# A startup ordered by hand for each engine up to the eighth decoded tile, with its loads in another order

## The chip, the cores and the metric

One core of one Trainium2 chip. The metric is the device time of one execution in microseconds; the median of several runs is compared. A profiled execution gives a trace of every instruction on TensorE (PE, with its weight loads PEld), VectorE (DVE), ScalarE (ACT), GpSimd (POOL) and SyncE (SP), whose queue issues most DMAs.

## What is computed

Packed attention (32 packs attend to 576 keys, then 576 queries attend to the 32 packed rows), then two feed-forward layers, Mish and ELU. In float32 with float64 weights:

```python
def sm_attn(qq, kk, vv):
    s = scale * np.matmul(qq, kk.transpose(0, 1, 3, 2))
    s = s - np.max(s, axis=-1, keepdims=True)
    a = np.exp(s)
    a = a / (np.sum(a, axis=-1, keepdims=True) + 1e-09)
    return np.matmul(a, vv)
p_packed = sm_attn(p, k, v)                 # q, k, v: (4, 8, 576, 64), p: (4, 8, 32, 64)
out = sm_attn(q, p_packed, p_packed)
...
x = attn_out.transpose(0, 2, 1, 3).reshape(2304, 512)
h = x @ w_in                                # 512 x 2048
g = h * np.tanh(sp)                         # sp = log1p(exp(h)), Mish
x = g @ w_out                               # 2048 x 512
...                                         # second layer: the same with ELU
```

## The kernel before

**Weights.** Weights arrive as pairs of 32-bit words, in raw tiles of 128 x 1024 words (512 KB). `decode` (L129) turns a tile into float32 in steps: s0 rebiases one word of each pair on ACT (L147), s1 to s3 shift and merge the bits on DVE (L150, L155, L160), s4 splits the result into a high part on ACT (L175, names ending in h) and a low part on DVE (L179, names ending in l). Each product is then three matmuls: high x high, high x low, low x high. Tiles of w1i, the first layer's first matrix, are not split: they go to w1v, and when a pair of them is done, POOL writes the pair to DRAM for later batches (L167).

**Attention.** Batch 0 runs in the startup, batches 1 to 3 between the matmuls of the batch ahead. The steps are: transposes of keys (hk, DVE L236), `scores1` (sc: PE L256, row maxima L270 on DVE, exponentials L276 on ACT), `transpose_a1` (ta: PE L300, copies L226), `packed` (pk: PE L325, then L338, L349 or L347, and L226 into pt), transposes of queries (hq, L236), and `scores2` (s2): PE L366, transposes L380, maxima and differences L387 and L388, exponentials L389 on ACT, sums and norms L393 to L396, transposes back L403, then the split into a2h (ACT L175) and a2l (DVE L177).

**Fold.** The packed rows are multiplied into the first weight matrix: `fold(b, c)` (PE L428, split by L175 and L179 into gh and gl) needs the four w1i tiles of column c and pt of batch b. It takes the place of the second attention product.

**First layer.** `gemm1` (L459 to L461, six matmuls of 288 columns a unit) multiplies folded weights by a2h and a2l; Mish is L468 on ACT, its split L469 on ACT and L470 on DVE; `gemm2` (L487 to L489, twelve matmuls a unit) multiplies by w1o and runs two units (LAG) behind. A batch has 32 units. Units 0 to 3 need fold column 0, units 4 to 7 column 1, units 8 to 15 both again for the other half of the tokens, units 16 to 19 column 2, units 20 to 23 column 3. Unit n of gemm2 needs w1o tile kk of its number in the same way (kk 0 to 7 in the first 16 units).

**What sets the order.** The framework schedules by priority: instructions have the priority of the order in which they are written, and an engine takes the ready one with the highest, by a model of their durations. Then each engine runs its list in order. In the startup the attention steps are put ahead by `high_priority(60)`, and `filler(m)` (L679) issues m decode steps between them, 65 in all (13 tiles). Behind the startup, `mixture1` writes for each unit gemm1, Mish, decode steps up to DEC1[0] + (i + 1) x DEC1[1] / 32 tiles, attention and fold steps, and gemm2. F0 lists the units at which batch 0's folds of columns 1, 2, 3 are begun. The order of the w1 tiles is `w1seq`: w1i column 0, then by ORD w1o 0, w1i column 1 rows 0, 2, 1, 3, w1o 2, 3, 1, then 4 to 7, then columns 2 and 3 each with its four w1o tiles. The second layer (`mixture2`) begins at about 500 us; its first eight tiles are decoded in mixture1 at PACE2 steps a unit.

**Loads.** p on ACT's queue, k on SP, q of heads 0 to 3 on ACT's queue (8 transfers), v of two groups, two tiles, v of the others, three tiles, q of the other heads on SP (8), four tiles; one more tile with each tile that filler begins.

## Time and profile before

| | before |
|---|---|
| median of 3 runs | 838.66 us (837.78 to 840.06) |
| profiled execution | 838.91 us, of which the span of the trace is 836.8 |
| PE busy | 778.2 us, 93% of the span |
| DVE busy | 438.1 us, 52% |
| ACT busy | 348.1 us, 42% |
| granted TensorE clock, mean | 0.958 |

A page of the profile gives the busy time of each engine, the span in 40 slices, the DMA queues, the chain of work that ended last, and the costliest groups of instructions. Of the first 5 slices (105 us) the page's PE line shows 3, 5, 3, 8 and 9 tenths. Beside the page the trace answers questions on stretches: busy time by window, instructions in order of time, groups of instructions by line, and waits. A line such as `68.47 0.40 PE L487 MATMUL ... [2.19 <-ACT w1oh L175]` reads: at 68.47 us, 0.40 us long, on PE, from line 487, after 2.19 us of idle time that ended when ACT's line 175 wrote w1oh.

### The profile page before, as it was taken

How to read it: one execution, taken by the hardware profiler on the slowest of the kernel's cores; microseconds unless marked ns; L12 is line 12 of the kernel's file. 1: busy time of each engine (PE TensorE's matmuls, PEld its weight loads, DVE VectorE, ACT ScalarE, POOL GpSimd, SP SyncE). 2: the span in 40 equal slices, each digit the busy share in tenths (PEclk: the TensorE clock that was granted, in tenths of full speed). 3: DMA queues.
4: the chain of work that ended last, by engine and by line, in shares of the span. 5: the costliest groups of instructions: out<-in, count | busy, mean ns of one | idle time of the engine just before them, and what ended most of it. 6: DMA issues, size and time to landing. Idle time of an engine off the chain costs nothing. (4 is left out here: it accounts for less than half of the span.)

```text
span 836.8 us, 12979 instructions
## 1 busy us (share of the span) xinstructions
PE 778.2 (93%) x5172; PEld 669.6 (80%) x5172; DVE 438.1 (52%) x860; ACT 348.1 (42%) x674; POOL 14.3 (2%) x30
## 2 busy tenths in 40 slices
PE   3538989999999999999988999999999999999997
PEld 3217969889898997999976887888888888888886
DVE  3889886833564236374359984423343334242342
ACT  1365755655363737474356543312232223221222
POOL 0000000000000000000000000000000000000000
PEclk8558989999999999999999999999999999999999
DMA  8994674263326235030045512200020001000000
GB/s 192 281 409 152 210 214 144 95 174 58 104 85 186 47 90 198 34 126 30 26 174 179 176 53 71 82 1 0 1 76 13 0 1 51 13 1 1 26 26 25
DMA packets 86043, 80.00 MB, mean 96 GB/s; under 512 B 63712, under 2 KB 68320, under 8 KB 85984
## 3 DMA queue, kind: packets, MB, share of 16 engines
q1 hardware_dynamic: 76704, 69.16, 26.9%
q0 software_dynamic: 2432, 8.91, 2.9%
q10 hardware_dynamic: 6848, 1.11, 0.9%
q8 instruction: 40, 0.66, 0.3%
q14 instruction: 19, 0.16, 0.1%
HBM read 65.54 MB, written 13.63 MB: 95 GB/s over the span
## 5 line engine op out<-in xcount | busy, mean ns | idle before, releaser
L488 PE MATMUL acc<-gl,w1oh 128*128 128x288 f32 x512 | 152.4, 300 | 1.4 <-DVE gl L470 1.3
L489 PE MATMUL acc<-gh,w1ol 128*128 128x288 f32 x512 | 151.7, 298 | 0.9 <-DVE w1ol L179 0.9
L487 PE MATMUL acc<-gh,w1oh 128*128 128x288 f32 x512 | 148.5, 299 | 2.2 <-ACT w1oh L175 2.2
L549 PE MATMUL h<-yh,w2ih 128*128 128x512 f32 (+1 forms) x320 | 117.8, 372 | 7.3 <-DVE t L555 5.8
L550 PE MATMUL h<-yl,w2ih 128*128 128x512 f32 (+1 forms) x320 | 119.3, 373 | 0.3 <-DVE yl L177 0.3
L551 PE MATMUL h<-yh,w2il 128*128 128x512 f32 (+1 forms) x320 | 119.0, 372 | 0.0
L572 PE MATMUL o<-w2oh,gh 128*128 128x512 f32 x288 | 112.4, 390 | 1.1 <-ACT ob L224 0.7
L573 PE MATMUL o<-w2ol,gh 128*128 128x512 f32 x288 | 112.2, 390 | 0.0
L574 PE MATMUL o<-w2oh,gl 128*128 128x512 f32 x288 | 108.2, 389 | 0.0
L470 DVE TENSOR_TENSOR gl<-t,gh 128x288 fp32r<-128x288 f32 x128 | 57.9, 454 | 94.5 <-ACT gh L469 93.8
L488 PEld LDWEIGHTS acc<-gl,w1oh 128*128 128x128 f32 x512 | 97.4, 190 | 7.1 <-DVE gl L470 3.7
L487 PEld LDWEIGHTS acc<-gh,w1oh 128*128 128x128 f32 x512 | 96.3, 191 | 6.2 <-ACT w1oh L175 2.4
L489 PEld LDWEIGHTS acc<-gh,w1ol 128*128 128x128 f32 x512 | 97.5, 191 | 3.9 <-issue 2.6
L553 ACT ACTIVATE t<-h 128x512 f32<-128x512 f32 (+1 forms) x80 | 42.3, 552 | 138.2 <-PE h L551 133.7
L554 DVE TENSOR_SCALAR t<-t 128x512 f32<-128x512 f32 (+1 forms) x80 | 31.4, 399 | 122.0 <-ACT t L553 121.5
L468 ACT ACTIVATE t<-h 128x288 f32<-128x288 f32 x128 | 52.2, 409 | 100.2 <-PE h L461 97.0
L459 PE MATMUL h<-a2h,gh 128*128 128x288 f32 x256 | 77.3, 304 | 16.9 <-ACT a2h L175 15.9
L460 PE MATMUL h<-a2l,gh 128*128 128x288 f32 x256 | 77.0, 301 | 1.4 <-DVE a2l L177 1.4
L175 ACT ACTIVATE gh<-t 128x512 fp32r<-128x512 f32 (+1 forms) x80 | 46.6, 587 | 73.9 <-DVE t L555 38.5
L461 PE MATMUL h<-a2h,gl 128*128 128x288 f32 x256 | 76.7, 301 | 0.0
L549 PEld LDWEIGHTS h<-yh,w2ih 128*128 128x128 f32 x320 | 60.7, 190 | 19.5 <-DVE t L555 7.4
L177 DVE TENSOR_TENSOR gl<-t,gh 128x512 fp32r<-128x512 f32 (+1 forms) x80 | 50.1, 636 | 39.2 <-ACT gh L175 38.5
(96 smaller groups left out, 1098.4 us busy)
## 6 DMA issues: line engine op xcount, KB each, us to landing
w1r<-w_dr SPq DMA_DIRECT2D x24, 512.0 KB, 4.3
raw_w1i<-in_moe_w_in_dram SPq DMA_DIRECT2D x16, 512.0 KB, 6.8
raw_w1o<-in_moe_w_out_dram SPq DMA_DIRECT2D x16, 512.0 KB, 8.3
raw_w2i<-in_moe_w_in_dram SPq DMA_DIRECT2D x16, 512.0 KB, 4.3
raw_w2o<-in_moe_w_out_dram SPq DMA_DIRECT2D x16, 512.0 KB, 4.6
k<-in_k_dram SPq DMA_DIRECT2D x16, 288.0 KB, 6.4
y_dr<-y POOLq DMA_DIRECT2D x16, 288.0 KB, 2.5
out_dram<-ob SPq DMA_DIRECT2D x18, 256.0 KB, 2.0
```

The lines of the kernel that those rows point to most:

```text
L459: nc.tensor.matmul(out=hp, lhsT=wh, rhs=xh, start=(kt == 0), stop=False)
L460: nc.tensor.matmul(out=hp, lhsT=wh, rhs=xl, start=False, stop=False)
L461: nc.tensor.matmul(out=hp, lhsT=wl, rhs=xh, start=False, stop=(kt == 1))
L487: nc.tensor.matmul(out=o, lhsT=wh[:, cs], rhs=gh, start=first, stop=False)
L488: nc.tensor.matmul(out=o, lhsT=wh[:, cs], rhs=gl, start=False, stop=False)
L489: nc.tensor.matmul(out=o, lhsT=wl[:, cs], rhs=gh, start=False, stop=last)
L549: nc.tensor.matmul(out=hp, lhsT=wh, rhs=xh, start=(i == 0), stop=False)
L550: nc.tensor.matmul(out=hp, lhsT=wh, rhs=xl, start=False, stop=False)
L551: nc.tensor.matmul(out=hp, lhsT=wl, rhs=xh, start=False, stop=(i == 3))
L572: nc.tensor.matmul(out=o, lhsT=gh[:, ts], rhs=wh, start=(kk == 0), stop=False)
L573: nc.tensor.matmul(out=o, lhsT=gh[:, ts], rhs=wl, start=False, stop=False)
L574: nc.tensor.matmul(out=o, lhsT=gl[:, ts], rhs=wh, start=False, stop=(kk == NK - 1))
```

## The change

- The startup is written inside `manual_schedule` for PE, DVE, ACT and SP: these engines take its instructions in the order in which they are written. `high_priority` and `filler` go. POOL is not in it.
- The order itself is written out. The transpose of p comes first on DVE, then keys, scores1 with both exponentials, and decode steps of tiles 0 to 3 (w1i column 0) between the steps of ta, pk and hq; then scores2; fold 0; tiles 4 to 7 (w1o 0 to 3) between and behind the norms.
- The tiles keep their plain order (no ORD): w1i column 0, w1o 0 to 3, w1i column 1, w1o 4 to 7, and so on. Eight are decoded in the startup, not 13.
- Loads: p on ACT's queue; then all on SP: k, all of v, four tiles, all of q, four tiles, two more.
- DEC1 goes from [14, 26] to [9, 38], F0 from [0, 12, 17] to [3, 12, 16], PACE2 from 9 to 10.
- `split` is divided into `split_hi` and `split_lo`, decode's s4 into s4 (high) and s5 (low). For batch 0 both a2h are written before both a2l. The instructions stay the same.

```diff
-    ORD=[4, 8, 10, 9, 11, 6, 7, 5, 12, 13, 14, 15],
-    DEC1=[14, 26],
-    F0=[0, 12, 17],
+    DEC1=[9, 38],
+    F0=[3, 12, 16],
...
-    PACE2=9,
+    PACE2=10,
...
             else:
+                split_hi(t.bitcast(F32), wt[key][0][:, r % 2, :], 1.0 / WSCALE)
+
+        def s5():
+            if not whole:
                 hi, lo = wt[key]
-                split(t.bitcast(F32), hi[:, r % 2, :], lo[:, r % 2, :], 1.0 / WSCALE)
-
-        return [s0, s1, s2, s3, s4]
+                split_lo(t.bitcast(F32), hi[:, r % 2, :], lo[:, r % 2, :], 1.0 / WSCALE)
+
+        return [s0, s1, s2, s3, s4, s5]
...
+        ] if b else [
+            lambda: exps(0),
+            lambda: exps(1),
+            lambda: (norm(0), back(0, 0)),
+            lambda: (norm(1), back(1, 0)),
+            lambda: (back(0, 1), back(1, 1)),
         ]
...
-    w1seq[4:16] = [w1seq[i] for i in ORD]
...
-        load_kt(q, qt_in, 0, 0, "q", nc.scalar)
-        load_vt(0, 0)
-        load_w1(2)
-        load_vt(0, 1)
-        load_w1(3)
-        load_kt(q, qt_in, 0, 1, "q")
+        for kt in range(2):
+            load_vt(0, kt)
         load_w1(4)
...
+        for kt in range(2):
+            load_kt(q, qt_in, 0, kt, "q")
+        load_w1(4)
+        load_w1(LEAD)
...
+        dec = [decode(*w1dec.popleft()) for _ in range(8)]
...
         order = [
-            hk[0][0], hk[1][0], hk[2][0], hk[3][0], sc[0][0], sc[0][1], sc[1][0], sc[1][1], 2, sc[0][2], sc[1][2],
-            ta[0][0], ta[0][1], ta[1][0], ta[1][1], 4, pk[0][0], pk[0][1], pk[0][2], pk[1][0], pk[1][1], pk[1][2],
-            6, hq[0][0], hq[1][0], hq[2][0], hq[3][0], s2[0], s2[1], s2[2], s2[3], s2[4], 8, f0[0], f0[1],
-            s2[5], s2[6], 45,
+            hk[0][0], hk[1][0], hk[2][0], hk[3][0], sc[0][0], sc[0][1], sc[1][0], sc[1][1],
+            *parts(0, 0), *parts(1, 0), sc[0][2], ta[0][0], ta[0][1], sc[1][2], ta[1][0], *parts(0, 1, 2),
+            ta[1][1], *parts(2, 0), *parts(3, 0), pk[0][0], *parts(0, 3, 4, 5), pk[0][1], pk[1][0], *parts(1, 1, 2), pk[0][2],
+            pk[1][1], *parts(1, 3, 4, 5), pk[1][2], *parts(2, 1, 2, 3, 4, 5), hq[0][0], hq[1][0], *parts(3, 1, 2, 3, 4, 5),
+            hq[2][0], hq[3][0], s2[0], s2[1], s2[2], f0[0], s2[3], s2[4], f0[1], *parts(4, 0), s2[5],
+            *parts(5, 0), s2[6], *parts(4, 1, 2, 3, 4), s2[7],
+            *parts(5, 1, 2, 3, 4), *parts(4, 5), *parts(6, 0), *parts(6, 1, 2, 3, 4), *parts(5, 5),
+            *parts(7, 0), *parts(7, 1, 2, 3, 4), *parts(6, 5), *parts(7, 5),
         ]
         for o in order:
-            if isinstance(o, int):
-                filler(o)
-            else:
-                with tc.high_priority(P['HP']):
-                    o()
-        while micro:
-            filler(1)
+            o()
...
-    startup()
+    with tc.manual_schedule(engines={e.engine for e in (nc.tensor, nc.vector, nc.scalar, nc.sync)}):
+        startup()
```

Here `parts(n, i, ...)` are the steps i of tile n, and `s2[7]` is the new last step of scores2 (both a2l).

## Rows read from the trace of the kernel before

**Rows 1.** Windows: window, length, busy (instructions) by engine, PEclk, DMA share, GB/s.

```profile
54.70:76.00 21.30, 16.69 (x88) 13.58 (x89) 21.30 (x41) 13.81 (x27) 1.63 (x2) 0.70 0.88 300
76.00:89.00 13.00, 13.00 (x122) 12.19 (x121) 12.65 (x28) 9.25 (x21) 0.54 (x1) 1.00 0.11 43
89.00:112.00 23.00, 22.99 (x203) 20.78 (x202) 19.06 (x43) 17.58 (x36) 0.64 (x2) 1.00 0.67 233
112.00:127.20 15.20, 11.57 (x140) 8.65 (x139) 11.07 (x24) 5.69 (x13) 0.96 (x2) 0.78 0.84 210
127.20:300.00 172.80, 171.69 (x1592) 153.52 (x1591) 87.36 (x187) 90.22 (x186) 4.33 (x8) 1.00 0.39 108
```

**Rows 2.** Timeline, 10 to 21 us: start, length, engine, line, operation, [idle before].

```profile
10.37 0.78 DVE L236 STREAM_TRANSPOSE kT<-k 128x576 f32<-128x576 f32 x1 [1.46 <-DMA k<-in_k_dram]
11.08 1.20 DVE L674 STREAM_TRANSPOSE pT<-pr 128x1024 f32<-128x1024 f32 x1
12.33 2.30 PE L256 MATMUL pm<-kT,pT 32*32 32x288 f32 x64 [5.01 <-DVE pT L674]
...
19.95 0.65 ACT L147 ACTIVATE raw_w1i<-raw_w1i 128x512 f32<-128x512 f32 x1 [17.92 <-DMA raw_w1i<-in_moe_w_in_dram]
20.63 0.43 DVE L150 TENSOR_SCALAR dec<-raw_w1i 128x512 int32<-128x512 int32 x1 [4.18 <-ACT raw_w1i L147]
```

**Rows 3.** Timeline, from the second scores to the first gemm2.

```profile
34.74 2.22 PE L366 MATMUL pm<-qT,pt 64*32 64x288 f32 x32 [5.61 <-DVE qT L236]
...
39.44 0.85 DVE L380 STREAM_TRANSPOSE x<-pm 128x288 f32<-128x288 f32 x2
...
47.12 1.41 DVE L393 TENSOR_REDUCE sm<-x 128x18 f32<-128x576 f32 x2 [3.47 <-ACT x L389]
...
58.01 0.76 DVE L177 TENSOR_TENSOR a2l<-a2t,a2h 128x576 fp32r<-128x576 f32 x1
...
63.62 0.55 PE L487 MATMUL acc<-gh,w1oh 128*128 128x288 f32 x2
```

**Rows 4.** Decode: groups by form up to 60 us; gl; windows of dec (DVE, ACT).

```profile
L155 DVE SCALAR_TENSOR_TENSOR dec<-raw_w1i,dec 128x512 int32<-128x512 int32 x8 | 5.4, 683 | 0.1
L160 DVE SCALAR_TENSOR_TENSOR w1v<-raw_w1i,dec 128x512 int32<-128x512 int32 x8 | 5.3, 683 | 0.0
L150 DVE TENSOR_SCALAR dec<-raw_w1i 128x512 int32<-128x512 int32 x8 | 3.3, 419 | 6.2 <-ACT raw_w1i L147 6.2
...
L179 DVE SCALAR_TENSOR_TENSOR w1ol<-dec,w1oh 128x512 fp32r<-128x512 f32 x1 | 0.7, 687 | 0.0
...
L470 DVE TENSOR_TENSOR gl<-t,gh 128x288 fp32r<-128x288 f32 x128 | 57.9, 454 | 94.5 <-ACT gh L469 93.8
...
0.00:60.00 60.00, 16.86 (x31) 0.61 (x1) 0.61 0.97 289
47.10:58.10 11.00, 4.93 (x9) 0.61 (x1) 0.50 1.03 406
```

**Rows 5.** SP's queue: two timeline rows, and what the first v waited for.

```profile
10.19 0.38 SPq L200 DMA_DIRECT2D v<-in_v_dram  x1
...
23.38 7.21 SPq L213 DMA_DIRECT2D q<-in_q_dram  x8
...
SPq L200 <- DMA pr<-in_p_dram: 7.6, 1, 7.6
```

**Rows 6.** Timeline of PE, a wait in gemm2 and the start of unit 4 of gemm1.

```profile
68.47 0.40 PE L487 MATMUL acc<-gh,w1oh 128*128 128x288 f32 x1 [2.19 <-ACT w1oh L175]
...
76.07 0.29 PE L459 MATMUL h<-a2h,gh 128*128 128x288 f32 x1
76.20 0.29 PE L460 MATMUL h<-a2l,gh 128*128 128x288 f32 x1
```

**Rows 7.** Timeline of PE, two neighbouring matmuls of gemm2 at 122 us.

```profile
122.03 0.44 PE L488 MATMUL acc<-gl,w1oh 128*128 128x288 f32 x1
122.27 0.44 PE L489 MATMUL acc<-gh,w1ol 128*128 128x288 f32 x1
```

More of the change, by code (lines that the diff above doesn't have):

```diff
@@ L31 @@
     EVA='va',
-    HP=60,
     WARM=16,
@@ L168, in s4, with split_hi, split_lo @@
             else:
+                split_hi(t.bitcast(F32), wt[key][0][:, r % 2, :], 1.0 / WSCALE)
+        def s5():
+            if not whole:
                 hi, lo = wt[key]
-                split(t.bitcast(F32), hi[:, r % 2, :], lo[:, r % 2, :], 1.0 / WSCALE)
-        return [s0, s1, s2, s3, s4]
-    def split(val, hi, lo, factor=1.0):
+                split_lo(t.bitcast(F32), hi[:, r % 2, :], lo[:, r % 2, :], 1.0 / WSCALE)
+        return [s0, s1, s2, s3, s4, s5]
+    def split_hi(val, hi, factor=1.0):
         nc.scalar.activation(out=hi, in_=val, func=ACTF.Copy, scale=factor)
+    def split_lo(val, hi, lo, factor=1.0):
         if factor == 1.0:
@@ L181, in split @@
             )
+    def split(val, hi, lo, factor=1.0):
+        split_hi(val, hi, factor)
+        split_lo(val, hi, lo, factor)
     def reload_w1i(c):
@@ L396, in norm, with back @@
             nc.vector.tensor_tensor(out=x[s], in0=x[s], in1=sm.to_broadcast([128, NB, NP]), op=ALU.mult)
-        def back(s):
+        def back(s, part=None):
+            if part == 1:
+                split_lo(x["t", s], *x["hl", s])
+                return
             if s == 0:
@@ L404, in back @@
             hi, lo = (y[b][:, s].rearrange("p e s -> p (e s)") for y in (A2h, A2l))
-            split(t, hi, lo)
+            split_hi(t, hi)
+            if part is None:
+                split_lo(t, hi, lo)
+            x["t", s], x["hl", s] = t, (hi, lo)
         return [
@@ L617 @@
     LAG = 2
-    ORD = P['ORD']
     def interleave(name):
@@ L666, in startup @@
             load_heads(k, kt_in, 0, g, "k", nc.sync)
-        load_kt(q, qt_in, 0, 0, "q", nc.scalar)
-        load_vt(0, 0)
-        load_w1(2)
-        load_vt(0, 1)
-        load_w1(3)
-        load_kt(q, qt_in, 0, 1, "q")
-        load_w1(4)
-        nc.vector.transpose(
-            out=pT.rearrange("p g x k -> p (g x k)"), in_=pr.rearrange("p g d -> p (g d)")
-        )
-        micro = deque()
-        def filler(m):
-            for _ in range(m):
-                if not micro and w1dec:
-                    micro.extend(next_w1())
-                    load_w1(1)
-                if micro:
-                    micro.popleft()()
+        for kt in range(2):
+            load_vt(0, kt)
+        load_w1(4)
+        for kt in range(2):
+            load_kt(q, qt_in, 0, kt, "q")
+        load_w1(4)
+        load_w1(LEAD)
         at = attention_steps(0)
@@ L690, in startup, with parts @@
         f0 = fold(0, 0)
-        order = [
-            hk[0][0], hk[1][0], hk[2][0], hk[3][0], sc[0][0], sc[0][1], sc[1][0], sc[1][1], 2, sc[0][2], sc[1][2],
-            ta[0][0], ta[0][1], ta[1][0], ta[1][1], 4, pk[0][0], pk[0][1], pk[0][2], pk[1][0], pk[1][1], pk[1][2],
-            6, hq[0][0], hq[1][0], hq[2][0], hq[3][0], s2[0], s2[1], s2[2], s2[3], s2[4], 8, f0[0], f0[1],
-            s2[5], s2[6], 45,
+        dec = [decode(*w1dec.popleft()) for _ in range(8)]
+        def parts(n, *which):
+            return [dec[n][i] for i in which]
+        nc.vector.transpose(
+            out=pT.rearrange("p g x k -> p (g x k)"), in_=pr.rearrange("p g d -> p (g d)")
+        )
+        order = [
+            hk[0][0], hk[1][0], hk[2][0], hk[3][0], sc[0][0], sc[0][1], sc[1][0], sc[1][1],
[6 more added lines that the diff above has]
+            *parts(7, 0), *parts(7, 1, 2, 3, 4), *parts(6, 5), *parts(7, 5),
         ]
         for o in order:
-            if isinstance(o, int):
-                filler(o)
-            else:
-                with tc.high_priority(P['HP']):
-                    o()
-        while micro:
-            filler(1)
+            o()
     class Track:
```

## The prediction

> **What bounds the kernel now.** I read the time by stages first. From 127.2 us to 300 us TensorE (PE) is busy for 171.69 of 172.80 us at the granted clock 1.00 [rows 1]: from there on the end is fixed by PE's work, which the change leaves as it is. (The one later edit, PACE2 from 9 to 10, goes with one more step for each decoded tile, so 9/5 = 1.8 tiles for each unit become 10/6 = 1.67, for eight tiles in all; I cost it at nothing, half a unit of PE cover.) So the change is worth what it moves PE's state at about 127 us, no more.
>
> Before that point the bound is VectorE (DVE). It is busy for 21.30 of 21.30 us from 54.7 to 76, for 12.65 of 13.00 to 89, then for 19.06 of 23.00 and 11.07 of 15.20 [rows 1]: no idle time up to 76, and 0.35 + 3.94 + 4.13 = 8.4 us from there to 127.2.
>
> Then I read the startup as a chain in order of time. Scores of batch 0 start at 12.33, behind the transposed packs pT at 11.08. DVE then loses 4.18 us at 20.63, in front of a decode step that waits for ScalarE (ACT), which had itself stood 17.92 us in front of the first weight tile [rows 2]. The second scores start on PE at 34.74 and last 2.22, to 36.96, but DVE transposes them only at 39.44; the row sums wait 3.47 us for the exponentials at 47.12; the second a2l ends at 58.01 + 0.76 = 58.77, and gemm2 (L487) starts at 63.62 [rows 3]. The reason is one: decode steps stand in the queues of ACT and DVE ahead of attention steps and wait for data. After the start PE is still held, 2.19 us at 68.47 by the high half of a w1o tile, and the fifth unit of gemm1 comes at 76.07 [rows 6].
>
> **The change part by part.** *Decode behind attention.* Up to the second a2l three losses go: 39.44 - 36.96 = 2.5 us of late transposes; the 3.47 in front of the row sums; and DVE's work for later tiles between 47.12 and 58.01. That last was 4.93 us in nine instructions on dec tiles; the new order keeps one tile there, 0.42 + 0.69 + 0.69 = 1.8, so 3.1 go [rows 4]. The sum is 2.5 + 3.5 + 3.1 = 9.1, and of it I give back 0.4 because f0[1], the split of the folded weights, now stands ahead of the norms and waits for its turn on ACT. The second a2l then ends at 58.77 - 8.7 = 50.1.
>
> *pT first.* The transpose of pr now heads DVE's order. The four key transposes, which ran before it, come after it, 4 x 0.7 = 2.8 us (0.78 each [rows 2], less the overlap of neighbours); three of them used to lie beside the loads. pT lasts 1.20 and starts between 10.2, where the third pr transfer had landed [rows 5], and 11.08 [rows 2], so the scores start between 14.2 and 15.1, not at 12.33; I take 14.6. The cover is the 4.18 us stall of rows 2, which goes, since both exponentials now precede the first decode step. If that cover failed, 1.9 to 2.8 us would be on the path.
>
> *Loads.* All sixteen q transfers go to SP's queue, behind four weight tiles; before, eight went out on ACT's queue. On SP eight of them took 7.21 us to issue at 23.38, and the first v, which waited 7.6 us for pr to land, was not issued before 10.19 [rows 5]. In the new order v follows k and can go in that gap, from 10.19 - 7.6 = 2.6 on, as transfers ahead of it land, so SP has 16 v, 4 tiles and 16 q to issue where it had 16 v, 5 tiles and 8 q from 10.19 to 23.38 + 7.21 = 30.6. Starting some 5 us earlier with seven more issues of 0.4 (a v) to 0.9 us (a q), it issues the last q between 28 and 32; scores2 starts between 32 and 35.5, against 34.74. I take no gain and no loss and keep -2.5 and +1 for the range. The Trainium skill (DMA: Bandwidth & Descriptors, Issuing engines are not separate DMA queues) says that transfers from several issuing engines run on the same 16 DMA engines, and that a second issuer saves only sequencer time; by it the transfers are not slower on one queue, and what the move costs is their issue time on SP, the 7.2 us of [rows 5], which is already in the count above.
>
> *The tail of the startup.* Behind the a2l steps DVE has, in the written order, three more tiles and four low halves: 3 x 1.8 + 4 x 0.69 = 8.2 [rows 4]; the three steps of a tile now follow each other directly, and each waits for the one before it to drain, which I put at 0.6 in all. If later steps don't slip in between, the first gl of gemm1's unit 0 (0.45 us [rows 4]) ends at 50.1 + 8.2 + 0.6 + 0.5 = 59.4, and gemm2 starts there: 63.62 - 59.4 = **4.2 us earlier**. Queued behind that tail on DVE and ACT are the Mish splits; PE waits for them with two units of gemm1 done.
>
> *What DVE owes then.* Up to 60 us DVE had done 31 decode instructions in 16.86 us, 0.54 each [rows 4]. The new order has done 8 x 3 + 4 = 28 by 58.9, and the same attention: three fewer, 1.6 us. So DVE stands at 58.9 where it stood at 60.0 - 1.6 = 58.4 before, **0.5 us behind**; what is earlier is PE alone, because the 28 are the urgent ones, while the 31 held steps of tiles that PE needed later. The lead of 4.2 us at gemm2 is borrowed: 4.2 + 0.5 = 4.7 us of DVE work comes later and has to fit into the 8.4 us of DVE idle time between 76 and 127.2 [rows 1].
>
> *w1o tiles 0 to 3 before w1i's second column.* The 2.19 at 68.47 goes, since all four are split before gemm2 starts. What is late instead is the fold of column 1: after 59.4 DVE has four tiles (7.2), three gl (1.4) and two splits of the fold (1.4), 10.0, and then there are some 1.5 us of PE and ACT in the chain, so unit 4 of gemm1 starts near 71 against 76.07, a lead of 5. After that four w1o tiles, each 1.8 + 0.69 = 2.5, gate units 4 to 7. I let the lead fall back to the 4.2 of gemm2's start.
>
> **The sum** is against the profiled execution: 836.8 us of span and 2.1 around it, 838.91, which is 0.25 above the median of 838.66. I take the lead off the median: 838.66 - 4.2 = 834.5 us.
>
> **The rivals.**
> A. *The larger lead is kept.* If Mish and its splits slip into the tail, the first gemm2 comes 8.7 earlier, not 4.2, and DVE's idle 8.4 can pay for it almost in full: 838.66 - 8.7 = 830, between 826 and 832. For it: in that tail ACT has two short steps for each tile where DVE has four. Against it: DVE has no idle time there to slip into.
> B. *DVE is the bound all the way.* The 4.7 owed do not fit, because idle time on DVE lies where it waits for PE or ACT. Then the 0.5 by which DVE is behind is all that is left: 839.2.
> E. *The early units run at half clock.* Consecutive matmuls of 288 columns start 76.20 - 76.07 = 0.13 us apart at the upper level of 2.4 GHz [rows 6] and 122.27 - 122.03 = 0.24 at the lower of 1.2 GHz, after the pauses of that stage [rows 7]; the granted clock is 0.70 from 54.7 to 76 and 0.78 from 112 to 127.2 [rows 1]. If PE pauses between its first units, the four units of 18 matmuls take 72 x 0.24 = 17.3 us from 59.4 on, and the fifth starts at 76.7 against 76.07: 839.3. The Trainium skill (TensorE: Matmul & The Clock Gate, HAM oscillation) has this as a rule: an array that keeps pausing for data falls back to the lower level.
> C. *Slower.* 24 tiles, not 19, are now decoded behind the startup, and within the first 20 units and not 23 (DEC1: 9 + 38/32 for each unit in place of 14 + 26/32). The last four w1o tiles, 4 x 2.5 = 10.0 us of DVE, are written before unit 20 of gemm1, which needs the fold of column 3. If all four do pass ahead of that fold, unit 20 starts 0.5 + 10.0 - 8.4 = 2.1 us later than before with all of DVE's idle time used, 840.8, and 10.5 later with none, 849; the middle is 845. With all idle time used it decides from the fourth such tile on (2.5 x 4 > 8.4 - 0.5), with 5 us of it used from the second. For it: DVE is the fullest engine there. Against it: gemm2 needs those tiles eight units later, and the order after the startup is made by priorities.
> D. *The order is kept but the loads are not in time.* q lands 3 us later, at 34 to 35; everything behind shifts by 2.5 to 3: 837.3.
>
> **How the numbers follow.** Forecast 834.5 (832 to 836): 0.40. A 0.19, B 0.10, C 0.18, D 0.07, E 0.06. Faster by over 0.3% (under 836.1; 0.3% is about what a measurement can tell from no change) is the forecast and A, 0.59. B, D, E and the near end of C are within 0.3%: 0.24. The rest of C is slower by over 0.3% (above 841.2): 0.17. The range leaves out the far part of C (0.13) and the lower end of A (0.05): 827 to 842.5.
>
> **What would show it.** Right: no DVE wait of 4 us near 20 us; the second a2l ends near 50; gemm2 starts near 59.4; unit 4 of gemm1 near 71; unit 20 four us before 127.2. Rival A shows a gemm2 start near 55; B has unit 20 within 1 us of 127.2; C a long PE wait in front of unit 20; D scores2 after 36; E a granted clock of 0.50 up to 76. Wrong altogether would be a second a2l later than 55, or a PE that idles after 127 where it did not.

## The result, and the profile after

The changed kernel takes 848.06 us (median of 4 runs, 847.22 to 849.71) against 838.60 for the kernel before (4 runs): a ratio of 1.0113, with a 95% interval of 1.0092 to 1.0134. It is 9.5 us slower where 4.2 faster was forecast, and lies outside the range given. Its profiled execution took 849.71 us, with a span of 847.7; that is 10.8 above the profiled execution of before.

The first view is the windows over the stretches of [rows 1] (columns as there), now of the changed kernel:

```profile
54.70:76.00 21.30, 13.39 (x72) 12.00 (x72) 20.64 (x39) 11.41 (x21) 0.59 (x1) 0.77 0.46 168
76.00:89.00 13.00, 9.66 (x66) 5.42 (x67) 12.90 (x26) 7.42 (x15) 0.70 (x2) 0.58 0.80 268
89.00:112.00 23.00, 23.00 (x196) 21.19 (x195) 21.31 (x50) 21.02 (x42) 1.06 (x2) 0.94 0.56 167
112.00:127.20 15.20, 12.98 (x139) 12.10 (x144) 14.81 (x31) 10.46 (x23) 1.29 (x2) 1.00 0.85 291
127.20:300.00 172.80, 166.72 (x1512) 147.32 (x1497) 86.01 (x183) 86.99 (x179) 4.34 (x8) 0.99 0.40 111
```

The second line differs most. From 76 to 89 us PE was busy throughout at clock 1.00 in [rows 1]; now it is busy for 9.66 of 13.00 us at 0.58. DVE, which had idle time there and behind it, has 0.10 us left in that line and 1.69 in the next. Behind 127.2 us PE, which was busy for 171.69 of 172.80 us, is busy for 166.72.

The second view is the timeline of the end of attention 0, which answers to [rows 3] (start, length, engine, line, operation, count, idle time before and its releaser):

```profile
37.25 2.18 PE L374 MATMUL pm<-qT,pt 64*32 64x288 f32 x32 [9.43 <-DVE qT L244]
...
45.42 0.65 ACT L145 ACTIVATE raw_w1i<-raw_w1i 128x512 f32<-128x512 f32 x1 [17.78 <-DMA raw_w1i<-in_moe_w_in_dram]
46.71 0.65 ACT L145 ACTIVATE raw_w1i<-raw_w1i 128x512 f32<-128x512 f32 x1 [0.64 <-DMA raw_w1i<-in_moe_w_in_dram]
47.27 1.24 ACT L397 ACTIVATE x<-x 128x576 f32<-128x576 f32 x2
...
49.02 0.69 DVE L183 SCALAR_TENSOR_TENSOR gl<-pm,gh 128x512 fp32r<-128x512 f32 x1 [5.70 <-ACT gh L177]
...
50.99 0.74 DVE L401 TENSOR_REDUCE sm<-x 128x18 f32<-128x576 f32 x1
...
58.28 1.42 DVE L181 TENSOR_TENSOR a2l<-a2t,a2h 128x576 fp32r<-128x576 f32 x2
```

The second a2l ends at 58.28 + 1.42 = 59.70 us, against 58.77 before and the 50.1 of the forecast. Two rebias of w1i tiles that are not in the hand-written order (the ninth and tenth, of column 1) stand on ACT ahead of the exponentials (47.27). They wait for their tiles until 45.42 and 46.71. DVE's next step in the order is the low half of the fold's split (f0[1]), which needs ACT's high half behind those exponentials: it idles for 5.70 us.

The third view is PE's and ACT's timeline where the time is lost:

```profile
78.34 1.96 PE L448 MATMUL pm<-w1v,pt 64*32 64x512 f32 x16 [3.35 <-DVE w1v L158]
81.08 0.61 PE L479 MATMUL h<-a2h,gh 128*128 128x288 f32 x1 [0.77 <-ACT gh L177]
```

```profile
134.83 0.67 ACT L145 ACTIVATE raw_w1o<-raw_w1o 128x512 f32<-128x512 f32 x1 [4.94 <-DMA raw_w1o<-in_moe_w_out_dram]
```

```profile
136.21 0.69 PE L355 MATMUL pm<-ident,pv 128*64 128x128 f32 x2 [4.13 <-DVE pv L346]
...
139.73 0.29 PE L507 MATMUL acc<-gh,w1oh 128*128 128x288 f32 x1
```

The fold of column 1 waits for its last decode step until 78.34, and unit 4 of gemm1 starts at 81.08 instead of 76.07 [rows 6]. Later ACT stands 4.94 us in front of a w1o tile, and PE 4.13 us behind that. Unit 32 of gemm1 starts at 173.34 against 160.17 before, 13.17 later. Summed over PE's matmuls from 48 us on (each to its end or to the next one's start), 25.14 - 15.03 = 10.11 us of this is idle time and 100.20 - 97.14 = 3.06 longer matmuls, those at the lower clock. The gap is still 13.16 when gemm3 starts (440.27 against 427.11) and 10.82 at its second block (530.20 against 519.38); that part was not pursued.

The forecast and rival B had taken unit 20 of gemm1 as the measure of PE's state near 127 us. Units 20 and 32 of the kernel before, then of the changed one:

```profile
127.21 0.29 PE L459 MATMUL h<-a2h,gh 128*128 128x288 f32 x1
...
160.17 0.42 PE L459 MATMUL h<-a2h,gh 128*128 128x288 f32 x2
```

```profile
128.59 0.40 PE L479 MATMUL h<-a2h,gh 128*128 128x288 f32 x1 [0.75 <-ACT gh L177]
...
173.34 0.42 PE L479 MATMUL h<-a2h,gh 128*128 128x288 f32 x2
```

Unit 20 comes only 1.38 us later; it doesn't show what PE still owes. By 127.2 us both traces have the 120 matmuls of units 0 to 19 of gemm1, but the kernel before has 221 matmuls of gemm2 and 410 of attention and folds, the changed one 192 and 361.

### The profile page after: what moved, and what is told of

It reads as the page before. It is cut to its first block, busy times and chain, and to the rows that moved or that the text cites. A ratio compares the mean times of both kernels' runs of the same rounds, so it can differ in the third digit from the quotient of the medians.

```text
span 847.7 us, 12973 instructions
## 1 busy us (share of the span) xinstructions
PE 780.4 (92%) x5172; PEld 670.9 (79%) x5172; DVE 441.6 (52%) x860; ACT 349.4 (41%) x674; POOL 14.3 (2%) x30
## 4 chain that ended last, share of the span: by engine, by line
PE 80%; DVE 7%; DMA 4%; ACT 3%; SPq 3%; issue 2%; ACTq 0%; DVEq 0%
PE h L570 7%; PE h L569 7%; PE h L571 7%; PE o L592 7%; PE o L593 7%; PE o L594 7%; PE acc L508 7%; PE acc L509 7%; PE acc L507 7%; PE h L479 4%; PE h L481 4%; PE h L480 4%; SPq L221 2%; PE pm L448 1%; DMA raw_w1i<-in_moe_w_in_dram 1%
## 5 line engine op out<-in xcount | busy, mean ns | idle before, releaser
L479 PE MATMUL h<-a2h,gh 128*128 128x288 f32 x256 | 79.9, 314 | 16.4 <-ACT a2h L177 13.7
L479 PEld LDWEIGHTS h<-a2h,gh 128*128 128x128 f32 x256 | 50.3, 197 | 27.5 <-ACT a2h L177 15.2
```

The costliest lines, as they stand in the source:

```text
L479: nc.tensor.matmul(out=hp, lhsT=wh, rhs=xh, start=(kt == 0), stop=False)
```

## The experiments

"Changed" is the changed kernel. Each run's median is followed by the 95% interval of its ratio to the kernel before, timed beside it; differences between runs are taken from the ratios (table below), as parts of 838.6 us. Theories are named as in the expectations.

**1. Pin the two rebias.** On changed; `dec` holds ten tiles.

```diff
             *parts(7, 0), *parts(7, 1, 2, 3, 4), *parts(6, 5), *parts(7, 5),
+            *parts(8, 0, 1, 2, 3, 4, 5), *parts(9, 0, 1, 2, 3, 4, 5),
```

> Edit: ten instead of eight tiles are decoded in the hand-written order; tiles 8 and 9 (w1i column 1) stand at its end, so that their rebias on ACT can't stand in front of the exponentials of attention 0 any more. Theory START (the chain of attention 0 was held and the rest of the loss follows from it): the two exponentials start near 42.5 to 43.5 us instead of 47.27 and 48, the second a2l ends near 55 to 56 instead of 59.70, unit 4 of gemm1 starts near 77 to 78 instead of 81.08, time 843 to 845. Rival DVE (work that DVE owes sets unit 4, whatever attention does): a2l earlier by as much, unit 4 within 1 us of 81.08, time 847 to 849. Rival PACE (the loss lies in the stretch of 100 to 140 us, where the decode follows the pace numbers): unit 4 may move, unit 32 stays within 1.5 us of 173.3, time 846.5 to 849.

845.61 us (1.0052 to 1.0099). The exponentials, the end of both a2l, unit 4's fold and unit 4 in this run's timeline:

```profile
40.70 0.68 ACT L397 ACTIVATE x<-x 128x576 f32<-128x576 f32 x1 [14.07 <-DVE x L396]
```

```profile
52.67 1.42 DVE L181 TENSOR_TENSOR a2l<-a2t,a2h 128x576 fp32r<-128x576 f32 x2
```

```profile
74.04 1.96 PE L448 MATMUL pm<-w1v,pt 64*32 64x512 f32 x16 [5.34 <-DVE w1v L158]
77.00 0.61 PE L479 MATMUL h<-a2h,gh 128*128 128x288 f32 x1 [1.00 <-ACT gh L177]
```

The exponentials come 6.6 us earlier, the second a2l ends at 54.09, gemm2 starts at 57.87 (forecast 59.4), and yet unit 4 starts 0.93 us later than before the change. So the held exponentials cost some 3 us: 1.0113 - 1.0076 is 3.1 us of time, with intervals that still touch, and unit 32 starts 3.2 us earlier than in changed. START held for unit 4, and for the time within 0.6 us; but 6.4 us of loss (1.0076) are left, which don't come from the held chain. A new thing shows: PE has done units 0 to 3 by 68.7, pauses 5.34 us ahead of the fold, and runs at clock 0.60 from 76 to 89.

**2, 3. q first; and q first, pins and a later f0[1] together.** q's sixteen loads ahead of the first four w1i tiles; in the second run with the edit of run 1 and f0[1] moved behind `s2[6]`.

> Edit: the sixteen loads of q are issued ahead of the first four w1i tiles instead of behind them. Theory START: scores2 starts at 33 to 34.5 instead of 37.25, but the exponentials still stand behind the rebias of tiles 8 and 9, whose loads are as late as now, so a2l ends within 1 us of 59.70 and the time is 846.5 to 849. A theory LOADS (late q alone made the loss): a2l near 56, time 843 to 845. Against both: w1i tiles 0 to 3 land 3 us later and DVE waits for them: time 848 to 851.

> Edit: the two edits of the runs before together (tiles 8 and 9 pinned behind tile 7, q ahead of w1i) and f0[1], the split of the first fold, behind both norms. Theory START: exponentials at 39.5 to 41, row sum right behind the first of them, second a2l near 51 to 53, gemm2 from 58 to 60, unit 4 near 75 to 77 instead of 81.08, and unit 32 moved as far: time 839 to 843. Rival DVE: a2l near 52, unit 4 within 1.5 us of 81.08: time 846 to 849. Rival PACE: unit 4 near 76 but unit 32 within 1.5 us of 173.3: time 846 to 849.

851.50 us (1.0120 to 1.0167) and 851.74 (1.0130 to 1.0170). Run 2 went as its last sentence says, a little beyond it. In run 3 no theory held; its DVE timeline shows why:

```profile
31.15 0.43 DVE L148 TENSOR_SCALAR dec<-raw_w1i 128x512 int32<-128x512 int32 x1 [10.17 <-ACT raw_w1i L145]
...
32.95 0.28 DVE L346 TENSOR_SCALAR pv<-pm,rs 128x64 f32<-128x64 f32 x1
```

The first decode step stands ahead of attention's pv in the fixed order, and now waits 10.17 us for its tile (10.11 in run 2); everything behind it waits too. What a fixed order gains depends on the landing time of each tile in it.

**4. Pace as before the change.** On changed: DEC1 14, 26; F0 1, 12, 17; PACE2 9.

> Edit: the beginning as changed, but the pace numbers as before the change (DEC1 14 and 26 instead of 9 and 38, PACE2 9 instead of 10, F0 1, 12, 17 instead of 3, 12, 16; F0 can't begin with 0 here since column 1 is decoded in unit 0). Theory START: the beginning is as late as now (a2l 59 to 60.5, unit 4 at 80 to 82), unit 32 within 2 us of 173.3, time 846 to 849. Rival PACE: the waits of 100 to 140 us fall back to what they were before the change (unit 16 to 20 of gemm2 without a wait of 5 us for a tile), unit 32 near 168, time 841 to 844.

852.60 us (1.0135 to 1.0181): unit 4 at 85.19, unit 32 at 174.50. Unit 32 is as START said, unit 4 and the time are as neither; the pace numbers of the change are the better ones for its beginning.

**5. Column 1 ahead of w1o 1 to 3.** Twelve tiles pinned, in the order w1o 0, column 1, w1o 1 to 3.

> Edit: the run that pinned tiles 8 and 9, and besides the four tiles of w1i column 1 stand right behind the first w1o tile in loads and decode (as in the kernel before), ahead of w1o 1 to 3; twelve tiles are pinned. Theory ORDER (unit 4 waits on DVE, which decodes column 1 only behind w1o 0 to 3): the fold of column 1 starts at 65 to 70 us instead of 74.04 in the run with tiles 8 and 9 pinned and 78.34 in the changed kernel, unit 4 of gemm1 at 67 to 72, the row of gemm2's unit 1 later by 3 to 5 us, unit 32 at 162 to 167 instead of 170.1, time 837.5 to 842.5. Rival PACE: unit 4 comes earlier as said, but the first unit of the second half of gemm2 (unit 16) still starts at 133 to 138 and unit 32 within 2 us of 170.1: time 843.5 to 847. Rival DVE total: column 1 earlier, but w1o 1 to 3 are later by as much, PE waits there instead; idle of PE from 48 us to unit 32 within 2 us of the 18.8 of that run: 843.5 to 847.

847.33 us (1.0053 to 1.0116). The fold starts at 67.56 as ORDER had it, but gemm2's unit 1 only at 69.92 and unit 4 at 79.04. PE's idle time from 48 us to unit 32 is 20.1 us against 18.8 in run 1: DVE total, with a time a little beyond it.

**6, 7, 12. The rest of the change without its beginning.** On the kernel before: its tile order ORD undone; the change's pace numbers; both.

```diff
-    ORD=[4, 8, 10, 9, 11, 6, 7, 5, 12, 13, 14, 15],
-    DEC1=[14, 26],
-    F0=[0, 12, 17],
+    ORD=[4, 5, 6, 7, 8, 9, 10, 11, 12, 13, 14, 15],
+    DEC1=[9, 38],
+    F0=[3, 12, 16],
...
-    PACE2=9,
+    PACE2=10,
```

> Edit on the kernel before: its tile order is undone (w1o 0 to 3 ahead of w1i column 1, as in the changed kernel), all else as before. Theory ORDER: the fold of column 1 and with it unit 4 of gemm1 come 4 to 7 us later than 76.07, unit 32 3 to 6 us later than 160.17: time 841.5 to 845. Rival (the work of DVE is the same, it is only paid elsewhere: w1o 1 comes earlier and the idle ahead of gemm2's unit 1, 2.19 and 0.94 us, goes): time 837.5 to 840.5.

> Edit on the kernel before: only the pace numbers of the change (DEC1 9 and 38, F0 3, 12, 16, PACE2 10). Theory PACE (a part of the loss lies there): PE waits of over 3 us appear between 116 and 140 us, unit 32 2 to 5 us later than 160.17, time 841 to 844.5. Rival START/ORDER (the pace numbers are worth nothing by themselves): unit 32 within 1.5 us of 160.17, time 837.5 to 840.5.

> Edit on the kernel before: tile order as in the changed kernel and its pace numbers, together; so all of the change but the beginning written by hand and its loads. Each alone came out 2 to 3.5 us faster than the kernel before. If they add up: 832.5 to 835.5, and what is left of the change (beginning and loads) costs 12.5 to 15.5 us. If both remove the same wait: 835.5 to 838.5. If they collide (column 1 decoded behind w1o 1 to 3 and fewer tiles ahead): 838.5 to 843.

836.42 us (0.9943 to 0.9977), 837.78 (0.9961 to 0.9993) and 834.87 (0.9931 to 0.9961). Run 6 is faster than either theory had it, and its unit 4 comes at 72.50, earlier and not later than 76.07. In run 7 unit 32 is 3.14 us later, as PACE said, with the time of the rival. The two add up in run 12: this part of the change is a gain of 0.54%, and the beginning alone costs 1.0113 - 0.9946 = 0.0167, which is 14.0 us (13.2 by the medians). The gain lies where I had costed nothing: in the third run unit 32 starts at 161.70, 1.5 later than before, and the time comes back in gemm3's first block and a half (427.11 to 562.90 us before, 428.63 to 559.52 in run 12). PE idles there for 2.8 us instead of 6.1, and its matmuls take 1.6 us less, at a granted clock of 0.99 instead of 0.97.

**8. f0[1] behind the norms,** on run 1.

> Edit: tiles 8 and 9 pinned behind tile 7, and f0[1] (the split of the first fold) behind the second norm instead of ahead of the first; loads as in the changed kernel. The row sum of the norm can then start when the second maximum is subtracted, near 43 us instead of 45.38, and the second a2l ends 1.5 to 2.5 us earlier than in the run with the pinned tiles alone. Theory DVE/ORDER: unit 4 of gemm1 waits on the decode of column 1, which is as late, so unit 4 at 76 to 78 and the time within 1.5 us of 845.6. Rival START: unit 4 and all behind it 2 us earlier: 842.5 to 844.

847.73 us (1.0055 to 1.0117). The second a2l ends at 57.31, not earlier but 3.2 later than in run 1, and unit 4 at 78.48. The place of f0[1] is not what the chain lost.

**9. Fill the pause.** Run 1, and 28 matmuls without use in front of the fold of column 1.

```diff
+            for i in range(FILL.get((b, c), 0)):
+                nc.tensor.matmul(out=ps[i % 2], lhsT=wt["w1o", 1][1][:, 1, 0:128], rhs=wt["w1o", 1][1][:, 1, :])
```

> Edit: the run with tiles 8 and 9 pinned, and 28 matmuls of 512 columns without use ahead of the fold of column 1, on the last w1o tile that gemm2's unit 3 needs, into the fold's own bank (which the fold's first matmuls overwrite). They fill the pause of TensorE between gemm2's unit 3 (ends near 69) and the fold (74.04). Theory CLOCK (the pause is free, since the fold waits for DVE, but it leaves the clock at 0.50 for units 4 to 7): the clock is 1.00 from 75 to 95 us, unit 4 stays at 76 to 78, unit 8 starts at 85 to 87 instead of 89.89, and time is 841 to 844 if that comes through. Rival ACT/DVE (what comes behind waits for the decode anyway): unit 8 is earlier by 3 to 4 us, but the first unit of the second half of gemm2 stays at 134.5 to 136.5 and unit 32 within 1 us of 170.11: time 844.5 to 847.

848.44 us (1.0098 to 1.0132). The windows of run 1 and of this run over 76 to 89 us, in this order:

```profile
76.00:89.00 13.00, 11.12 (x76) 8.73 (x75) 12.68 (x26) 8.59 (x19) 0.00 (x0) 0.60 0.58 179
```

```profile
76.00:89.00 13.00, 10.95 (x98) 9.04 (x96) 13.00 (x29) 10.91 (x23) 0.77 (x1) 1.00 0.60 191
```

The clock is back at 1.00 and unit 8 starts at 84.34 instead of 89.89, near the 83.72 of before. By unit 16 the gain is gone (113.49; run 1 111.57); on the way PE waits 2.1 us for DVE's gl and 1.6 for ACT's Mish, where run 1 has no such wait. The rival ACT/DVE comes nearest, with a time 1.4 us beyond it. The Trainium skill (TensorE: Matmul & The Clock Gate, HAM oscillation — how this bites in real kernels) says that an array that keeps pausing for data falls to the lower clock and pays for it in the work behind; these two runs agree on the clock, 0.60 and 1.00, and not on the price: the time didn't fall.

**10. Every second rebias on POOL,** on run 1, for the tiles from column 1 on.

> Edit: the run with tiles 8 and 9 pinned, and every second rebias of the tiles from w1i column 1 and w1o 5 on (12 of 24) goes to POOL instead of ACT, which takes some 8 us (12 by 0.67) off ACT between 70 and 150 us. Theory ACT (ACT has the rebias and splits that it did by 60 us in the kernel before still ahead of it, and is busy all of 100 to 120): ACT's busy share in 100 to 120 falls, the pauses of TensorE at 121 to 126 us shrink, unit 32 comes 3 to 6 us earlier than 170.11: time 839.5 to 843. Rival DVE (DVE has as much ahead of it): unit 32 within 1.5 us of 170.11, time 844 to 847. A rebias on POOL that takes over 2 us each or holds DVE back would make it slower: 847 to 852.

856.20 us (1.0169 to 1.0215). One group of POOL in the view by lines (busy, mean ns | idle before):

```profile
L146 POOL TENSOR_SCALAR raw_w1i<-raw_w1i 128x512 f32<-128x512 f32 x6 | 9.9, 1654 | 21.3 <-DMA raw_w1i<-in_moe_w_in_dram 21.2
```

A rebias of w1i takes 1.65 us there against 0.68 on ACT in the same run, and the tiles come late (the fold of column 3 starts at 130.80, in run 1 at 123.47); ACT's load stays untested.

**11. The same beginning without the fixed order.**

```diff
-    with tc.manual_schedule(engines={e.engine for e in (nc.tensor, nc.vector, nc.scalar, nc.sync)}):
-        startup()
+    startup()
```

> Edit: the changed kernel without the fixed order: the same steps, loads and numbers in the same written order, but the scheduler is free to place them on each engine. Theory PIN (the fixed order keeps decode out of the idle time that DVE and ACT have while attention 0 waits): DVE and ACT are busy in 20 to 60 us as in the kernel before (ACT some 19 to 20 us instead of 11.4), second a2l at 58 to 62, unit 4 of gemm1 at 72 to 77, unit 32 at 159 to 164: time 835 to 840. Rival LOADS (v and q behind each other on SP's queue make the loss): unit 32 within 3 us of 173.3: time 845 to 849.

849.94 us (1.0111 to 1.0142). PIN falls in time, though unit 4 comes at 73.00 as it said. The scheduler decodes earlier (the sixteenth tile at 78 us, in changed at 87), the second a2l comes at 66.19, and unit 32 at 171.00, where LOADS has it; but run 16 shows the loads by themselves to cost nothing. Run 13, below, also decodes eight tiles in a beginning without a fixed order, and is 10.1 us faster (1.0007 against 1.0127). It differs from this run in the order as written, with attention put ahead by priority, and in the loads. That is a comparison of two kernels and no single edit.

**13, 16, 18. One part of the beginning at a time,** on the run of 834.87 us: the last filler with 20 or 70 steps instead of 45 (8 or 18 tiles decoded instead of 13); the loads in the order of the change.

```diff
-            s2[5], s2[6], 45,
+            s2[5], s2[6], 20,
```

> Edit on the kernel before with the change's tile order and pace numbers (834.87 us): the last filler of the beginning runs 20 steps instead of 45, so that the beginning decodes 8 tiles as in the changed kernel instead of 13, and leaves the rest to the units. Theory COUNT (the units bring tiles 8 to 12 too late): column 1 is decoded 3 us or more later than 68 us, unit 4 of gemm1 at 77 to 81 instead of 73.67, time 838 to 845. Rival (the scheduler places them the same, since DVE is free for them in the same places): unit 4 within 2 us of 73.67, time 833.5 to 837.

> Edit on the kernel before with the change's tile order and pace numbers (834.87 us): the loads of the beginning in the order of the change (v, four w1i tiles, all of q on SP, then w1o), nothing else. Theory LOADS (the load order is the larger part of the 13 us): scores2 2 to 4 us later than in that kernel, second a2l at 60 to 64, unit 4 of gemm1 at 78 to 81, time 842 to 848. Rival ORDER OF STEPS (the steps as written, not the loads, make it): unit 4 within 2 us of 73.67, time 834 to 838.

> Edit on the kernel before with the change's tile order and pace numbers (834.87 us): the last filler of the beginning runs 70 steps instead of 45, so that it decodes 18 tiles instead of 13. Theory COUNT (each tile taken out of the units' way pays): 832 to 834.5. Rival (5 tiles were enough to cover the units up to 4; more stands in the way of their splits on DVE): 834.5 to 838.

8 tiles: 840.80 us (0.9990 to 1.0024), 5.1 more than with 13; unit 4 comes at 76.86, at the edge of what COUNT said. 18 tiles: 846.50 (1.0058 to 1.0110), 11.6 more. Of the three counts 13 is the best, and neither theory of the last run holds; with 18, unit 4 waits for the splits of its fold behind decode:

```profile
77.10 0.40 PE L459 MATMUL h<-a2h,gh 128*128 128x288 f32 x1 [2.76 <-ACT gh L175]
80.62 0.85 PE L461 MATMUL h<-a2h,gl 128*128 128x288 f32 x2 [2.41 <-DVE gl L179]
```

With the old beginning the load order of the change costs nothing: 834.72 us (0.9918 to 0.9968). The run also bears on the premise of my forecast. The first row of gemm1 in the run of 834.87 and in this one:

```profile
54.04 0.85 PE L459 MATMUL h<-a2h,gh 128*128 128x288 f32 x2 [12.96 <-ACT a2h L175]
```

```profile
58.82 0.85 PE L459 MATMUL h<-a2h,gh 128*128 128x288 f32 x2 [19.71 <-ACT a2h L175]
```

Attention 0 ends 1.6 us later (second a2l 64.71 against 63.12), gemm1 starts 4.8 us later, and the time is the same. What is left for the loss of the beginning is the order of steps, the count of tiles and the fixed order, not the loads. From 76 to 89 us both keep PE busy for 13.00 us at clock 1.00, as the kernel before did.

**14, 17. Two repairs of the changed kernel.** Run 14 is run 1 with the k transposes of attention 1 queued on DVE behind column 1's last decode step. Run 17 pins thirteen tiles and decodes tiles 4 to 6 inside the waits of attention 0:

```diff
-            hq[2][0], hq[3][0], s2[0], s2[1], s2[2], f0[0], s2[3], s2[4], f0[1], *parts(4, 0), s2[5],
...
+            hq[2][0], hq[3][0], s2[0], *parts(4, 0), s2[1], *parts(4, 1, 2, 3, 4), s2[2], f0[0], *parts(5, 0), s2[3],
+            *parts(5, 1, 2, 3, 4), *parts(4, 5), s2[4], *parts(6, 0), *parts(6, 1, 2, 3, 4), *parts(5, 5), f0[1], s2[5],
...
```

> Edit on the changed kernel with tiles 8 and 9 pinned (845.6 us): the four transposes of attention 1's k on DVE are queued behind the last decode step of column 1 (they ran at 55 to 58 us, ahead of it). Theory KT (DVE sets unit 4, and these 2.8 us of it are not needed yet): column 1 decoded at 71 to 72 instead of 74, unit 4 of gemm1 at 73.5 to 75 instead of 77.00, time 841.5 to 843.5. Rival (attention 1 is what comes last behind unit 8, and it starts later by this edit): unit 4 earlier as said, the second maximum of attention 1 not earlier than 98 us, time 844.5 to 848.

> Edit on the changed kernel (848.06 us): thirteen tiles instead of eight stand in the hand-written order, tiles 4 to 6 are decoded in the waits of attention 0 (between the parts of scores2, the exponentials and the norms) instead of behind its second norm, tiles 8 to 12 at the end. Theory OWED (DVE's and ACT's decode, not attention 0, sets unit 4 of gemm1 and all behind it): the second a2l comes later than in the run with tiles 8 and 9 pinned (57 to 61 instead of 54), yet column 1 is decoded at 68 to 71 us instead of 74, unit 4 at 72 to 76 instead of 77.00, time 836 to 842. Rival CHAIN (attention 0's end sets it): unit 4 at 78 to 82 with the later a2l, time 846 to 850. Rival LATER (what differs lies behind unit 8, in how the scheduler places attention 1): unit 4 earlier as said, time 843.5 to 847.

847.06 us (1.0052 to 1.0110) and 847.29 (1.0066 to 1.0126). In 14 column 1 was decoded 1.3 us earlier than in run 1 (72.62 against 73.90), yet unit 4 came at 78.33, later than there:

```profile
77.17 0.63 ACT L178 ACTIVATE w1oh<-dec 128x512 fp32r<-128x512 f32 x1 [8.71 <-DVE dec L159]
77.70 0.58 ACT L178 ACTIVATE gh<-pm 128x512 fp32r<-128x512 f32 x1
```

```profile
78.33 0.61 PE L481 MATMUL h<-a2h,gh 128*128 128x288 f32 x1 [3.61 <-ACT gh L178]
```

On ACT the split of a w1o tile stands ahead of the split of the fold. It waits 8.71 us for DVE's decode, which now stands behind the four moved transposes (72.54 to 75.29). So run 14 put a new wait in the place of the old one and doesn't decide KT. In 17 unit 4 came at 75.37 with an a2l at 60.03, as OWED said (though column 1 was decoded only at 72.38), and the time did not follow: LATER, and a little beyond it (the profiled execution, 843.08, is the fastest of five; the others lie from 846.84 to 847.69).

**15. v of attention 1 on POOL's queue,** on the run of 834.87 us.

> Edit on the kernel before with the change's tile order and pace numbers (834.87 us): attention 1's v is loaded through POOL's queue instead of SP's. On SP eight of its loads wait from 76 to 90 us for the buffers that the second scores of attention 1 set free, and the four w1i tiles of column 3, which are queued behind them, go out at 95 to 98. Theory VSLOT (this wait holds the decode of column 3): column 3 goes out some 10 us earlier, unit 24 of gemm1 1 to 3 us earlier than 135.51, time 832 to 834.5. Rival (DVE is full and takes column 3 no earlier): time 834 to 836. Against: POOL's queue holds the stores of the decoded columns behind the waiting v loads, reloads come later: 836 to 840.

836.39 us (0.9938 to 0.9973). The first tile of column 3 is decoded at 102.5 us instead of 107.4, and unit 24 is not earlier (137.21 against 135.51): that wait is covered. The time is that of run 12 within the intervals.

**All kernels in one table,** read from the timelines, in us: end of the second a2l, starts of units 0, 4 and 8 of gemm1, of the second maximum of attention 1 on DVE, of unit 32, and the ratio to the kernel before.

```
kernel                  a2l    u0     u4     u8   max(1)    u32   ratio
before                58.77  54.76  76.07  83.72   93.65  160.17  1.0000
changed               59.70  54.62  81.08  94.24  103.41  173.34  1.0113
 1 pins               54.09  49.01  77.00  89.89   99.38  170.11  1.0076
 2 q first            61.02  55.95  84.32  96.20  107.10  175.45  1.0143
 3 q, pins, f0[1]     61.98  55.73  83.06  96.55  106.04  175.62  1.0150
 4 pace of before     58.96  53.88  85.19  97.15  109.01  174.50  1.0158
 5 column 1 first     54.27  49.20  79.04  92.74  103.18  170.94  1.0084
 8 pins, f0[1]        57.31  51.07  78.48  92.20  102.03  171.42  1.0086
 9 pins, fill         52.91  47.83  75.65  84.34   98.76  170.67  1.0115
10 pins, POOL         53.60  48.52  77.99  94.75  106.34  176.65  1.0192
11 not fixed          66.19  59.99  73.00  87.79  101.30  171.00  1.0127
14 pins, kT           54.85  49.77  78.33  92.17  101.88  172.25  1.0081
17 mixed              60.03  54.34  75.37  86.85   98.66  167.94  1.0096
 6 before, order      61.95  52.87  72.50  82.36   92.54  162.09  0.9960
 7 before, pace       61.02  57.00  79.43  87.07   96.13  163.31  0.9977
12 before, both       63.12  54.04  73.67  83.54   93.38  161.70  0.9946
13 12 with 8 tiles    64.26  53.87  76.86  86.05   96.41  166.74  1.0007
15 12, v on POOL      60.90  51.83  71.46  81.33   91.19  160.48  0.9955
16 12, loads          64.71  58.82  74.61  84.89   94.36  161.96  0.9943
18 12 with 18 tiles   61.46  52.39  77.10  93.43  102.16  170.13  1.0084
```

Down the columns, the correlation with the ratio is -0.42 for the second a2l and -0.23 for unit 0; the four kernels with the earliest a2l take 845.6 to 856.2 us. It is 0.62 for unit 4, 0.81 for unit 8 and 0.92 for attention 1's second maximum. But the table mixes two beginnings. Among the nine kernels with a fixed order and neither a fill nor POOL's rebias (changed, 1 to 5, 8, 14, 17) it is 0.79 for the second a2l and 0.82 for unit 0. So the end of attention 0 goes with the time among these nine, and doesn't tell one beginning from the other. What does is the stretch from unit 4 to unit 8: 7.6 to 10.3 us in every kernel up to a ratio of 1.0007, 11.5 to 16.8 in all slower ones but run 9 (8.69, with the clock at 1.00). These are correlations and no experiments. Of the edits, run 1 ends attention 0 5.6 us earlier and gains some 3 us; run 16, with the old beginning, ends it 1.6 us later and loses nothing.

## Why the prediction was wrong

**Decode behind attention** (second a2l at 50.1). It ended at 59.70. The written order holds its own steps in sequence but keeps no later step out: two rebias went ahead of the exponentials and held them for 5.4 us (from 41.87, when DVE had their input ready, to 47.27), and without them it ended at 54.09 (run 1). I had read the order of the diff as the order on the engine.

**The sum itself failed deeper.** I counted the late transposes (2.5 us) and the 3.47 us of [rows 3] as time that the chain could have for nothing. The kernel before decodes in it:

```profile
36.79 0.69 DVE L155 SCALAR_TENSOR_TENSOR dec<-raw_w1i,dec 128x512 int32<-128x512 int32 x1
...
38.27 0.43 DVE L150 TENSOR_SCALAR dec<-raw_w1i 128x512 int32<-128x512 int32 x1 [0.79 <-ACT raw_w1i L147]
38.73 0.69 DVE L155 SCALAR_TENSOR_TENSOR dec<-raw_w1i,dec 128x512 int32<-128x512 int32 x1
...
43.20 0.66 ACT L147 ACTIVATE raw_w1i<-raw_w1i 128x512 f32<-128x512 f32 x1 [2.15 <-DMA raw_w1i<-in_moe_w_in_dram]
44.59 0.65 ACT L147 ACTIVATE raw_w1o<-raw_w1o 128x512 f32<-128x512 f32 x1 [0.73 <-DMA raw_w1o<-in_moe_w_out_dram]
45.86 0.65 ACT L147 ACTIVATE raw_w1o<-raw_w1o 128x512 f32<-128x512 f32 x1 [0.62 <-DMA raw_w1o<-in_moe_w_out_dram]
46.42 1.24 ACT L389 ACTIVATE x<-x 128x576 f32<-128x576 f32 x2
```

While the transposes stand late, DVE works on w1i tiles, with one wait of 0.79 us. The 3.47 us are idle time of DVE, but in them ACT rebiases tiles for later, and waits for their loads. The change sends this work behind attention, where DVE was full already (21.30 of 21.30 us, [rows 1]).

**What DVE owes** (0.5 us behind at 60) is the step that failed most. The forecast has 28 decode instructions done by 58.9 us, where the kernel before had 31 in 16.86 us by 60 [rows 4]. The same window in the changed kernel, then in run 1 (dec tiles on DVE and on ACT):

```profile
0.00:60.00 60.00, 9.34 (x16) 0.63 (x1) 0.61 0.89 271
```

```profile
0.00:60.00 60.00, 11.31 (x19) 1.24 (x2) 0.63 0.90 272
```

DVE is 7.5 us of decode behind in the changed kernel and 5.6 in run 1; the eighth tile, due by 58.9, is through the shifts of the decode at 71.43 and 65.14. For all of DVE's work, the windows 20 to 40 and 40 to 60 us of the kernel before, of changed and of run 1, where the third of the busy times is DVE's and the fourth ACT's:

```profile
20.00:40.00 20.00, 10.98 (x141) 5.62 (x141) 15.83 (x36) 7.86 (x17) 1.22 (x2) 0.50 1.00 272
40.00:60.00 20.00, 3.83 (x12) 2.94 (x12) 16.53 (x33) 12.02 (x20) 0.33 (x1) 0.50 1.03 410
```

```profile
20.00:40.00 20.00, 8.13 (x131) 4.51 (x136) 13.40 (x28) 3.86 (x8) 1.29 (x2) 0.50 0.89 243
40.00:60.00 20.00, 2.66 (x22) 1.42 (x7) 13.23 (x25) 7.58 (x12) 0.00 (x0) 0.59 1.00 398
```

```profile
20.00:40.00 20.00, 8.39 (x136) 4.23 (x134) 14.28 (x30) 3.52 (x8) 1.28 (x2) 0.53 0.95 262
40.00:60.00 20.00, 7.35 (x30) 6.65 (x31) 17.65 (x31) 10.29 (x19) 0.00 (x0) 0.57 0.97 381
```

In busy time DVE is 32.36 - 26.63 = 5.7 us behind in the changed kernel, and unit 4 comes 5.0 late. In run 1 it is 0.4 behind, since k transposes of attention 1 and Mish's low halves ran in place of decode; unit 4 comes 0.9 late. So up to unit 4 DVE is the bound, as in rival B, with the 0.5 us mis-sized. Behind unit 4 that doesn't carry the loss: run 11 has 38 decode instructions by 60 us and still takes 849.94. I looked at DVE alone: ACT is 19.88 - 11.44 = 8.4 us behind at 60, and is busy 21.02 of 23.00 us from 89 to 112, where it had 17.58 [rows 1]. Whether that sets anything stays open.

**The tail, and w1o before column 1** (gemm2 at 59.4, unit 4 near 71, the lead falling by 0.8 us to unit 8). Run 1 had gemm2 at 57.87 and unit 4 at 77.00. That gemm2 came near its forecast is luck: the a2l was 4.0 us later than forecast, and from its end to gemm2 it was 3.8 us, in run 1 and in changed, and not 9.3. Later steps did slip into the tail, which was rival A's condition; but the k transposes of attention 1 were among them, 2.8 us that I had not counted, and the rest of the tail then stood ahead of column 1. Units 4 to 7, which took 83.72 - 76.07 = 7.65 us before, took 13.16 in changed and 12.89 in run 1: 5.5 and 5.2 us lost where the forecast let 0.8 go. With the clock at 1.00 they took 8.69 (run 9).

**Loads.** scores2 started at 37.25, behind the forecast's 32 to 35.5, as rival D has it (after 36); run 16 shows that this costs nothing with the old beginning, where decode fills the wait. **pT first** was right, in the number and in the cover: scores1 at 14.44 for 14.6, and no DVE wait of 4 us near 20 us.

**Rival E** was placed wrongly. The granted clock up to 76 us was 0.77, above the 0.70 of before; the pause came ahead of unit 4, and the lower clock behind it, 0.58 from 76 to 89. Longer matmuls are 3.06 us of the 13.17 at unit 32.

**Rival C** had the sign and the size (840.8 to 849), not the mechanism: PE waited 0.75 us in front of unit 20, which came 1.38 late. What was late is gemm2 and attention 1, with a wait of ACT for a tile's load at 130 to 135, and unit 16 of gemm2 at 139.73 for 121.63. Both signs of "wrong altogether" were there: the a2l at 59.70, and PE idle behind 127.

**What stays open.** Of the 14.0 us of the beginning, some 3 are the held exponentials (run 1), and 5.1 appear with the old beginning by the count of tiles alone (run 13), though adding tiles to the fixed order (run 17) does not give them back. The traces differ in how the steps of units 4 to 16 and of attention 1 stand among decode steps; no run here isolates that. So the cause of what is left is not shown, nor that these parts add up.

## What to carry to other kernels

Time in which a chain waits is a loss only if the engine that it waits for has nothing else to do; where decode for later units runs in it, pushing that decode behind the chain moves the bound, it doesn't remove it. Ask of a hand-written order what may still slip between its steps and which step waits on a transfer: one late tile stopped DVE for 5.7 us in the changed kernel and 10.2 in run 3. When an earlier start only lets PE reach the next gate sooner, it buys a pause and, behind that, the lower clock (5.34 us and 0.60 in run 1). And one unit of one product is a poor measure of where an engine stands: unit 20 was 1.38 us late, and unit 32 then 13.17. Of the kernels tried, the one with the change's tile order and pace numbers and the old beginning is the best: 834.87 us, a ratio of 0.9946 to the kernel before (0.9931 to 0.9961), and as good with the change's loads (834.72).

## What the hardware showed that I had not expected

The rebias of a 128x512 tile, a multiply of every second word, took 1.65 us on POOL (mean of 6) and 0.68 on ACT in the view by lines of run 10; spans on POOL are rough, but with 12 of them the time rose by 9.7 us over run 1. With 28 matmuls of no use in the pause (6.53 us in PE's timeline) the granted clock was 1.00 from 76 to 89 us, where it had been 0.60 without them.
